# First row tile loaded in two column halves, and the imaginary operand's first piece put ahead of the second row tile

## The chip, the cores and the metric

The kernel runs on one core of one Trainium2 chip. The metric is the device time of one execution in microseconds. All inputs and outputs are fp32 and lie in the chip's memory (HBM) when the kernel starts.

## The reference

```python
xn = _layernorm(x, axis=-1)                    # x: 2048 x 640, normalised along each row
a = jnp.einsum("bsd,ed->bse", xn, dft_hid_re)  # DFT along the hidden dimension
b = jnp.einsum("bsd,ed->bse", xn, dft_hid_im)
s = jnp.einsum("ts,bse->bte", dft_seq_re, a) - jnp.einsum("ts,bse->bte", dft_seq_im, b)
g = _silu((_silu(xn @ w_gate) * (xn @ w_up)) @ w_down)   # 640 -> 1536 -> 640
return x + s * g
```

The sequence matrices are 2048 x 2048, the hidden ones 640 x 640.

## The kernel before

The work is three chains of matrix products. `seq` multiplies the two sequence matrices with the normalised rows, `hid_s` multiplies what comes out with the hidden matrices, and `gate_up` and `down` do the feed-forward part. All large products are built with Strassen's scheme of seven half-size products. Each fp32 operand is split into a high part, written by ScalarE (ACT), and a low part, the rest, written by VectorE (DVE). A product of a 128 x 128 weight tile and 128 x 512 moving columns is then three fast passes on TensorE (PE): high by high, high by low, low by high.

A planner (`Plan`) sets the order of the instructions. Each piece of work is given with a due time, the buffers that it reads and writes, and a cost. `schedule` turns this into one list in order of time, and each engine gets its instructions in that order. For the opening the due times are written out by hand, in the tables `OPEN_DMA`, `OPEN_LN`, `OPEN_T` and `OPEN_S` (lines 730 to 739), as us from the start of the real work.

The opening (`opening`, line 855) is the part the change touches. It computes the first of the seven products for the real and for the imaginary sequence matrix at once, over eight row tiles of x (128 rows by 640 columns each). For each row tile kk there are two blocks of products, one with the real operand (i = 0) and one with the imaginary (i = 1). The left operands come in pieces of 512 KB, each for two row tiles. This text calls the row tiles x0, x1, x2 and so on (320 KB each), and the pieces re0, re1 (real, for row tiles 0 and 1, then 2 and 3) and im0, im1 (imaginary). In `OPEN_DMA` a single number is a row tile and a pair is a piece: `(0, 0)` is re0, `(1, 0)` is im0, `(0, 1)` is re1.

What happens to a row tile: two statistics on DVE, one for each half of its columns (`bn_stats`, in the profile BATCH_NORM_STATS2), their aggregate, a root on ACT, some small steps on DVE (all in `layer_norm`), the normalisation on ACT (xn<-xn), and the split of its columns into high (ACT, hl<-xn) and low parts (DVE, hl<-xn). The operand pieces are split too (hl<-raw, ACT and DVE). Row tile 0 is an exception: its products are done in full precision without a split (PE ps<-raw and ps<-raw,xn), two instructions each. Six such instructions use re0 and six use im0, and then row tile 1 begins with split operands (PE ps<-hl), 18 products for each row tile. Before all this PE runs eleven products on a tile of zeros (`busy`, ps<-z) as filler.

All loads of the opening are issued by SyncE (SP) on one queue. Eight completion semaphores are used in turn, so each transfer issues only when the eighth before it has landed. In the order of before, SP's issue for x5 waits for re0, the next ones wait for x1, im0, x2, x3 and re1 in that order.

Each engine's instruction is recorded by one helper, so nearly all have the line number L82.

Of the kernel before, what the change touches and what calls it, by code (L numbers as in the profile page):

```python
# [14 lines left out]
P = 128  # L15
# [263 lines left out]
def tile_fnet_swiglu(  # L279
# [16 lines left out]
    nc = Probe(tc.nc)  # L296
# [5 lines left out]
    pl = Plan()  # L302
    mv = one.tile([P, NS, 2], F32, name="mv")
    sm = one.tile([P, 6, NS], F32, name="sm")
    bst = one.tile([P, 2, 2, 6], F32, name="bst")
# [9 lines left out]
    def raw(name, a=0, n=None):  # L315
        o, (arena, size) = where[name], pl.size[name]
        n = size - a if n is None else n
        over = arena == "raw" and o >= RAW_KB * 256 - 8
        return space["raw3" if over else arena][:, o + a - over * (RAW_KB * 256 - 8):][:, :n]
# [235 lines left out]
    xn = pl.buf(("xn",), "raw2", NS * D)  # L555
# [5 lines left out]
    def xn_tile(k):  # L561
        return space["xn", k // 8][:, k % 8 * D:k % 8 * D + D]

    def load_x(k, lead, eng):
        pl.prod(lead, lambda: eng.dma_start(xn_tile(k), x[k * P:(k + 1) * P, :]), [], [(xn, k)])

    def layer_norm(k0, n, lead, root, stats, small):

        for k in range(k0, k0 + n):
            for h in range(2):
                pl.prod(stats[k - k0], lambda k=k, h=h: nc.vector.bn_stats(
                    bst[:, k % 2, h], xn_tile(k)[:, h * 320:h * 320 + 320]), [(xn, k)], [("bst", k % 2, h)])
            pl.prod(stats[k - k0], lambda k=k: nc.vector.bn_aggr(
                mv[:, k], bst[:, k % 2].rearrange("p a b -> p (a b)")),
                [("bst", k % 2, 0), ("bst", k % 2, 1)], [("mv", k)])
        y, t, mr, v, nm = (sm[:, i, k0:k0 + n] for i in range(5))
        mean, var = (mv[:, k0:k0 + n, i] for i in range(2))  # L580
        r = rowst[:, 0, NS + k0:NS + k0 + n]
        key = ("sm", k0)
        if small is nc.vector and n == 1:
            sign, half = (-1.0, nm) if k0 == 0 else (1.0, r)
            ops = [
                lambda: nc.scalar.activation(t, var, AF.Sqrt, bias=sm[:, 5, 4:5], scale=0.25),
                lambda: nc.gpsimd.tensor_scalar(v, var, EPS, 0.25 * sign, op0=ALU.add, op1=ALU.mult),
                lambda: small.reciprocal(y, t),
                lambda: small.scalar_tensor_tensor(v, v, y, t, op0=ALU.mult, op1=ALU.subtract if k0 == 0 else ALU.add),
                lambda: small.reciprocal(half, v),  # L590
            ]
            if k0:
                ops.append(lambda: small.scalar_tensor_tensor(mr, mean, -1.0, r, op0=ALU.mult, op1=ALU.mult))
        elif small is nc.vector:
            stt = small.scalar_tensor_tensor
            ops = [
                lambda: nc.scalar.activation(t, var, AF.Sqrt, bias=sm[:, 5, :1]),
                lambda: small.reciprocal(y, t),
                lambda: stt(t, var, EPS, y, op0=ALU.add, op1=ALU.mult),
                lambda: stt(t, t, -0.5, y, op0=ALU.mult, op1=ALU.mult),  # L600
                lambda: stt(r, t, 1.5, y, op0=ALU.add, op1=ALU.mult),
                lambda: stt(mr, mean, -1.0, r, op0=ALU.mult, op1=ALU.mult),
            ]
        else:
            ops = [
                lambda: small.tensor_scalar(v, var, EPS, 1.0, op0=ALU.add, op1=ALU.mult),
                lambda: small.tensor_tensor(y, v, sm[:, 5, 8:8 + n], op=ALU.pow),
                lambda: small.tensor_scalar(nm, mean, -1.0, 0.0, op0=ALU.mult, op1=ALU.add),
                lambda: small.tensor_tensor(t, v, y, op=ALU.mult),
                lambda: small.tensor_tensor(t, t, y, op=ALU.mult),  # L610
                lambda: small.tensor_scalar(t, t, -0.5, 1.5, op0=ALU.mult, op1=ALU.add),
                lambda: small.tensor_tensor(r, y, t, op=ALU.mult),
                lambda: small.tensor_tensor(mr, nm, r, op=ALU.mult),
            ]
        for i, fn in enumerate(ops):
            pl.prod(root[i > 0], fn, [("mv", k) for k in range(k0, k0 + n)], [key])
        if k0 == 0:
            neg = pl.buf(("neg",), "raw", 256)
            minus = lambda to, a, n, scale: small.tensor_scalar(to, xn_tile(0)[:, a:a + n], mean, scale, op0=ALU.subtract, op1=ALU.mult)
            for e in range(2):  # L620
                pl.prod(root[2], lambda e=e: minus(raw(neg, e * P, P), e * P, P, nm), [(xn, 0), key], [(neg, 0)])
            pl.prod(root[2], lambda: small.tensor_scalar(r, nm, -1.0, 0.0, op0=ALU.mult, op1=ALU.add), [key], [key])
            pl.prod(root[2], lambda: minus(xn_tile(0)[:, TC:], TC, P, r), [(xn, 0), key], [(xn, 0, 2)])
            pl.prod(root[2], lambda: small.tensor_tensor(mr, mean, nm, op=ALU.mult), [key], [key])
            pl.prod(lead[0], lambda: nc.scalar.activation(
                xn_tile(0)[:, :TC], xn_tile(0)[:, :TC], AF.Identity, bias=mr, scale=r), [key, (xn, 0), (neg, 0)], [(xn, 0, 0), (xn, 0, 1)])
            return neg
        for k in range(k0, k0 + n):
            pl.prod(lead[k - k0], lambda k=k: nc.scalar.activation(
                xn_tile(k), xn_tile(k), AF.Identity, bias=sm[:, 2, k:k + 1], scale=rowst[:, 0, NS + k:NS + k + 1]),  # L630
                [key, (xn, k)], [(xn, k, c) for c in range(3)])
# [96 lines left out]


    OPEN_DMA = ((0,), (0, 0), (1,), (1, 0), (2,), (3,), (0, 1), (1, 1), (4,), (5,), (0, 2), (1, 2), (6,), (7,), (0, 3), (1, 3))  # L730
    OPEN_LN = ((0, 1, (-2.5,), (-1.4, -1.0, -0.5), (0.4,)),
               (1, 1, (0.5,), (1.6, 1.9), (2.8,)),
               (2, 1, (3.5,), (5.0, 5.3), (6.1,)),
# [8 lines left out]
    def seq(k):  # L742
# [112 lines left out]
        def opening():  # L855
# [3 lines left out]
            at = lambda t: -t  # L859
# [7 lines left out]
            def fetch(i, g, t, a=None):  # L867
                src = cs[j, i, g // 2, :, 2 * (g % 2):2 * (g % 2) + 2]
                name = left[i, g]
                if a is None:  # L870
                    pl.prod(at(t), lambda: nc.sync.dma_start(wide(raw(name)), src), [], [(name, 0), (name, 1)])
                else:
                    pl.prod(at(t), lambda: nc.sync.dma_start(raw(name, a * TC, TC), src[:, a]), [], [(name, a)])

            t = -6.0
            for what in OPEN_DMA:
                if len(what) == 1:
                    load_x(what[0], at(t), nc.sync)
                else:
                    fetch(what[0], what[1], t, *what[2:])  # L880
                t += 0.45
            neg = [layer_norm(k0, n, [at(x) for x in apply], [at(x) for x in root], [at(x) for x in stats], nc.vector)
                   for k0, n, stats, root, apply in OPEN_LN][0]
            for kk in range(1, 8):
# [9 lines left out]
            for kk in range(8):  # L894
                for i, banks, db in part if kk < 7 else part[::-1]:
# [6 lines left out]
                    o, a = (s[i, 1], 0) if kk == 1 else (s[i, kk // 2 * 2], kk % 2)  # L902
# [23 lines left out]
        def p2(g):  # L926
            if fresh:
                for kk in (8 + 2 * g, 9 + 2 * g):
                    load_x(kk, 40 + 2 * g, nc.sync)
                layer_norm(8 + 2 * g, 2, *LEAD["xn", 4 + g], nc.gpsimd)  # L930
            return operand("p2", g, load(12, g, 11 if fresh else 20, "raw"))
# [19 lines left out]
        if fresh:  # L951
            opening()
        elif not shared:
            run(("p1", p1, b2, (1, 1)))
# [467 lines left out]
```

## Time and profile before

| | |
|---|---|
| median of 3 runs | 969.66 us (969.62 to 969.9) |
| profiled execution, its own time | 969.83 us |
| span in it | 967.6 us |
| TensorE busy | 961.7 us, 99% of the span |
| VectorE, ScalarE, GpSimd busy | 734.6, 488.6, 121.3 us |
| granted TensorE clock | 0.999 |
| first real product | 6.46 us |

All times in the text are us from the start of the span unless it says otherwise. The profile's matmul rows overlap, since a product starts while the one ahead of it drains, so waits on TensorE are read from the spacing of starts. In the timeline a row gives start, length, engine, line and operation, the tiles written and read, and a count; a bracket gives the idle time of the engine ahead of the row and what ended it.

### The profile page before, as it was taken

The page shows a single profiled execution, that of the slowest core. Times are in us where ns is not written, and L with a number is a line of the kernel's source. Part 1 is how long each engine was busy: PE and PEld are TensorE (multiplying, and loading weights), DVE is VectorE, ACT ScalarE, POOL GpSimd, SP SyncE. Part 2 cuts the span into 40 slices and gives each one's busy share as a digit, 9 for nine tenths or more (in the row PEclk, how much of TensorE's full clock was granted, in tenths as well). Part 3 has the DMA queues.
Part 4 walks back from the last instruction along what each step waited for, and adds up shares of the span by engine and source line. Part 5 has one row for each costly group of instructions (what it writes and reads, how often), then busy time and mean ns, then how long its engine had stood idle before and what let it go on. Part 6 is the DMA issues. An engine that isn't in the chain of part 4 may idle for free.

```text
span 967.6 us, 11521 instructions
## 1 busy us (share of the span) xinstructions
PE 961.7 (99%) x4235; PEld 792.0 (82%) x4235; DVE 734.6 (76%) x932; ACT 488.6 (50%) x676; POOL 121.3 (13%) x184
## 2 busy tenths in 40 slices
PE   9999999999999999999999999999999999999998
PEld 5888888888888888888888888888888888888887
DVE  7889668757774687676987898999978666666775
ACT  5686445454545455544356555563446444444341
POOL 1460211011101110111100211210002000000000
PEclk9999999999999999999999999999999999999999
DMA  9997848494938497778673374439699330105793
GB/s 352 283 249 215 233 147 229 152 271 106 231 109 255 109 236 263 208 196 253 170 213 131 141 265 155 168 136 289 222 292 256 99 133 4 55 1 163 240 346 131
DMA packets 64056, 186.50 MB, mean 193 GB/s; under 512 B 6528, under 2 KB 10368, under 8 KB 64000
## 3 DMA queue, kind: packets, MB, share of 16 engines
q1 hardware_dynamic: 45952, 125.45, 39.0%
q0 software_dynamic: 18048, 60.32, 24.2%
q8 instruction: 33, 0.54, 0.2%
q14 instruction: 23, 0.19, 0.1%
HBM read 151.39 MB, written 34.36 MB: 192 GB/s over the span
## 4 chain that ended last, share of the span: by engine, by line
PE 99%; DMA 0%; DVE 0%; ACT 0%; issue 0%; DVEq 0%; ACTq 0%
PE ps L82 99%; DMA xn<-in_x 0%; DVE raw L82 0%; DVE bst L82 0%; DVE sm L82 0%; ACT raw L82 0%; ACT sm L82 0%; DVE mv L82 0%; DVEq L82 0%; ACTq L82 0%
## 5 line engine op out<-in xcount | busy, mean ns | idle before, releaser
L82 PE MATMUL ps<-hl 128*128 128x512 f32 (+1 forms) x3258 | 780.1, 388 | 0.0
L82 PEld LDWEIGHTS ps<-hl 128*128 128x128 f32 x3258 | 610.1, 188 | 126.6 <-DVE hl L82 0.6
L82 DVE TENSOR_TENSOR hl<-raw,hl 128x1024 fp32r<-128x1024 f32 (+5 forms) x360 | 346.5, 994 | 134.3 <-ACT hl L82 94.4
L82 ACT ACTIVATE hl<-raw 128x1024 fp32r<-128x1024 f32 (+6 forms) x416 | 325.0, 826 | 170.3 <-DVE raw L82 84.8
L82 PE MATMUL ps<-hl,hl 128*128 128x512 f32 (+1 forms) x954 | 259.9, 388 | 0.0
L82 ACT ACTIVATE raw<-ps 128x512 f32<-128x512 f32 (+1 forms) x144 | 97.9, 681 | 231.4 <-PE ps L82 225.2
L82 PEld LDWEIGHTS ps<-hl,hl 128*128 128x128 f32 x954 | 179.0, 188 | 36.9
L82 DVE TENSOR_TENSOR raw<-raw 128x1024 f32<-128x1024 f32 (+7 forms) x216 | 178.6, 849 | 19.8 <-ACT raw L82 15.5
L82 DVE TENSOR_TENSOR raw<-ps,raw 128x512 f32<-128x512 f32 (+1 forms) x95 | 77.2, 814 | 48.4 <-PE ps L82 47.6
L82 DVE TENSOR_TENSOR raw<-raw,raw 128x512 f32<-128x512 f32 (+3 forms) x50 | 44.2, 892 | 6.5 <-ACT raw L82 4.3
L82 ACT ACTIVATE hl<-xn 128x1024 fp32r<-128x1024 f32 (+3 forms) x61 | 42.2, 723 | 13.6 <-PE ps L82 9.1
L82 POOL DMA_DIRECT2D p_dram<-raw x24 | 16.4, 686 | 251.4 <-DVE raw L82 215.7
L82 ACT ACTIVATE raw<-raw 128x512 f32<-128x512 f32 (+1 forms) x30 | 21.5, 718 | 46.7 <-DVE raw L82 46.7
L82 DVE TENSOR_TENSOR hl<-xn,hl 128x1024 fp32r<-128x1024 f32 (+3 forms) x50 | 40.8, 833 | 4.0 <-PE ps L82 3.9
L82 POOL DMA_DIRECT2D raw<-in_cs x36 | 32.5, 984 | 57.7 <-DMA raw<-in_cs 29.1
L82 DVE SCALAR_TENSOR_TENSOR hl<-raw,hl 128x256 fp32r<-128x256 f32 (+4 forms) x56 | 32.7, 586 | 4.0 <-ACT hl L82 4.0
L82 POOL DMA_DIRECT2D out<-raw x10 | 6.9, 689 | 226.6 <-DVE raw L82 197.3
L82 POOL DMA_DIRECT2D d_p<-hl x28 | 15.2, 543 | 71.4 <-ACT hl L82 59.6
L82 ACT ACTIVATE xn<-xn,sm,rowst 128x640 f32<-128x640 f32 (+1 forms) x16 | 14.1, 906 | 5.3 <-DVE sm L82 3.6
L82 DVE BATCH_NORM_STATS2 bst<-xn 128x6 f32<-128x320 f32 x32 | 13.7, 479 | 4.0 <-DMA xn<-in_x 4.0
L82 POOL DMA_DIRECT2D y_dram<-raw x12 | 8.2, 683 | 64.6 <-DVE raw L82 46.2
L82 POOL DMA_DIRECT2D raw<-p_dram x8 | 10.1, 1267 | 44.7 <-DVE raw L82 26.3
(42 smaller groups left out, 84.3 us busy)
## 6 DMA issues: line engine op xcount, KB each, us to landing
raw<-in_cs SPq DMA_DIRECT2D x84, 512.0 KB, 7.0
hl<-d_p SPq DMA_DIRECT2D x56, 384.0 KB, 5.0
raw<-in_cs POOLq DMA_DIRECT2D x36, 512.0 KB, 9.8
raw<-in_wb SPq DMA_DIRECT2D x24, 640.0 KB, 4.7
d_p<-hl POOLq DMA_DIRECT2D x28, 384.0 KB, 4.0
p_dram<-raw POOLq DMA_DIRECT2D x16, 512.0 KB, 4.4
raw<-p_dram SPq DMA_DIRECT2D x8, 768.0 KB, 8.5
xn<-in_x SPq DMA_DIRECT2D x16, 320.0 KB, 9.8
```

The lines of the kernel that those rows point to most:

```text
L82: return real(*args, **kw)
```

## The change

It does two things, both in the opening. x0 is loaded by two transfers, columns 0 to 319 and columns 320 to 639, and each of its two statistics depends on its own half alone; whatever else reads x0 depends on both. And in `OPEN_DMA` im0 moves ahead of x1, and re1 ahead of x3.

```diff
+    pl.alias[xn, 0] = [(xn, 0, "a"), (xn, 0, "b")]
...
+    def load_x(k, lead, eng, h=None):
+        if h is None:
+            pl.prod(lead, lambda: eng.dma_start(xn_tile(k), x[k * P:(k + 1) * P, :]), [], [(xn, k)])
+        else:
+            pl.prod(lead, lambda: eng.dma_start(xn_tile(k)[:, h * 320:h * 320 + 320], x[k * P:(k + 1) * P, h * 320:h * 320 + 320]),
+                    [], [(xn, k, "ab"[h])])
...
-                    bst[:, k % 2, h], xn_tile(k)[:, h * 320:h * 320 + 320]), [(xn, k)], [("bst", k % 2, h)])
+                    bst[:, k % 2, h], xn_tile(k)[:, h * 320:h * 320 + 320]), [(xn, k) if k else (xn, k, "ab"[h])], [("bst", k % 2, h)])
...
-    OPEN_DMA = ((0,), (0, 0), (1,), (1, 0), (2,), (3,), (0, 1), (1, 1), (4,), (5,), (0, 2), (1, 2), (6,), (7,), (0, 3), (1, 3))
+    OPEN_DMA = ((0,), (0, 0), (1, 0), (1,), (2,), (0, 1), (3,), (1, 1), (4,), (5,), (0, 2), (1, 2), (6,), (7,), (0, 3), (1, 3))
...
+                if len(what) == 1 and what[0] == 0:
+                    for h in range(2):
+                        load_x(0, at(t + 0.2 * h), nc.sync, h)
```

On SP, at the start of the program, the order changes as follows. `xn_108<-in_x` is a row tile (128x320 is one of x0's halves) and `raw<-in_cs` a piece of a left operand; lines with a minus are before's, with a plus the change's, the others stand in both.

```order
-L82 DMA xn_108<-in_x 128x640
+L82 DMA xn_108<-in_x 128x320 x2
+L82 DMA raw<-in_cs 128x1024 x2
+L82 DMA xn_108<-in_x 128x640 x2
 L82 DMA raw<-in_cs 128x1024
 L82 DMA xn_108<-in_x 128x640
 L82 DMA raw<-in_cs 128x1024
-L82 DMA xn_108<-in_x 128x640 x2
-L82 DMA raw<-in_cs 128x1024 x2
```

Read from the top, SP issued x0, re0, x1, im0, x2, x3, re1, im1; now it issues x0's two halves, re0, im0, x1, x2, re1, x3, im1. There is one transfer more, so every later one takes the next semaphore in turn, and each still waits for the eighth ahead of it: im1 for x0's first half, x4 for its second.

On DVE, at the start of the program, no instruction moves. Only what the first statistics wait for changes; the names in the brackets are the semaphores of SP's transfers by their turn (DMAHW0, DMAHW1) and of the engines.

```order
 L82 BN_STATS bst<-xn_108 128x6 [waits DMAHW0_49]
-L82 BN_STATS bst<-xn_108 128x6
+L82 BN_STATS bst<-xn_108 128x6 [waits DMAHW1_49]
 L82 BN_AGGR mv<-bst 128x2 [waits DVE_49]
 L82 RECIPROCAL sm<-sm 128x1 [waits Activation_49]
```

The first statistic now waits for x0's first half alone and the second for the second half. The rest of DVE's order and that of ACT, PE and GpSimd stand as they were.

More of the change, by code (lines that the diff above doesn't have):

```diff
@@ L562, in xn_tile @@
         return space["xn", k // 8][:, k % 8 * D:k % 8 * D + D]
-    def load_x(k, lead, eng):
-        pl.prod(lead, lambda: eng.dma_start(xn_tile(k), x[k * P:(k + 1) * P, :]), [], [(xn, k)])
+    pl.alias[xn, 0] = [(xn, 0, "a"), (xn, 0, "b")]
[5 more added lines that the diff above has]
+                    [], [(xn, k, "ab"[h])])
     def layer_norm(k0, n, lead, root, stats, small):
@@ L876, in opening @@
             for what in OPEN_DMA:
-                if len(what) == 1:
+                if len(what) == 1 and what[0] == 0:
+                    for h in range(2):
+                        load_x(0, at(t + 0.2 * h), nc.sync, h)
+                elif len(what) == 1:
                     load_x(what[0], at(t), nc.sync)
```

## The prediction

> **What bounds the kernel now.** I read the page first: the span, the busy times and the chain that ended last.
>
> ```profile
> span 967.6 us, 11521 instructions
> PE 961.7 (99%) x4235; PEld 792.0 (82%) x4235; DVE 734.6 (76%) x932; ACT 488.6 (50%) x676; POOL 121.3 (13%) x184
> ```
>
> Then the chain in order of time. It shows one serial piece before TensorE takes over for good, and nothing but TensorE up to the last results:
>
> ```profile
> 0.73 3.01 DMA xn<-in_x
> 3.76 0.90 DVE bst L82 x2
> 6.06 0.36 DVE raw L82
> 6.46 956.86 PE ps L82 x4224
> ```
>
> The first row tile (x0) lands at 0.73 + 3.01 = 3.74, its two statistics take 0.90, and the first real product starts at 6.46. A chain hides short gaps, so next come the timeline of TensorE (start, length, count) and that of its weight loads, where a bracket gives the idle time ahead of the row and what ended it:
>
> ```profile
> 1.31 4.87 PE L82 MATMUL ps<-z 128*128 128x512 bf16 x11 [1.31 <-POOL sm L82]
> 16.06 367.63 PE L82 MATMUL ps<-hl 128*128 128x512 f32 x1620
> ...
> 6.46 0.30 PEld L82 LDWEIGHTS ps<-raw 128*128 128x128 f32 x2 [1.19 <-DVE raw L82]
> 7.85 0.19 PEld L82 LDWEIGHTS ps<-raw,xn 128*128 128x128 f32 x1 [0.24 <-issue]
> 8.28 0.19 PEld L82 LDWEIGHTS ps<-raw,xn 128*128 128x128 f32 x1 [0.24 <-issue]
> 9.25 0.30 PEld L82 LDWEIGHTS ps<-raw 128*128 128x128 f32 x2 [0.78 <-DMA raw<-in_cs]
> 11.93 4.09 PEld L82 LDWEIGHTS ps<-hl 128*128 128x128 f32 x18 [0.24 <-DVE hl L82]
> 16.42 0.76 PEld L82 LDWEIGHTS ps<-hl 128*128 128x128 f32 x4 [0.40 <-DVE hl L82]
> ```
>
> From 16.06 on, 1620 products take 367.63 us, 0.227 each with no room for a wait, and the same pace holds to the end by the 99%. So TensorE loses time in three places only, all in the opening: until 6.46 (x0's chain), at 9.25 (the first imaginary operand, im0) and at 16.42 (DVE's low part of the second real operand, re1). Full-precision loads stand 8.28 - 7.85 = 0.43 apart, and six of them are one half of row tile 0: 6 x 0.43 = 2.57, but 9.25 - 6.46 = 2.79, so the wait for im0 costs 0.22, not the 0.78 in the bracket. What matters for the end is one number: when the load now at 16.42 can issue. Every us there is a us at the end.
>
> Next the queue. SP issues each transfer after the eighth before it has landed, so from the ninth on its issue times give landings:
>
> ```profile
> 1.63 0.42 SPq L82 DMA_DIRECT2D xn<-in_x  x1
> 2.10 0.43 SPq L82 DMA_DIRECT2D raw<-in_cs  x1
> ...
> 5.26 0.48 SPq L82 DMA_DIRECT2D xn<-in_x  x1
> 6.87 0.33 SPq L82 DMA_DIRECT2D raw<-in_cs  x1
> 9.22 0.33 SPq L82 DMA_DIRECT2D raw<-in_cs  x1
> 10.25 0.33 SPq L82 DMA_DIRECT2D xn<-in_x  x1
> 11.00 0.33 SPq L82 DMA_DIRECT2D xn<-in_x  x1
> 12.24 0.33 SPq L82 DMA_DIRECT2D raw<-in_cs  x1
> ```
>
> In order: re0 landed at 5.26, x1 at 6.87, im0 at 9.22, x2 at 10.25, x3 at 11.00, re1 at 12.24. All was issued long before it landed, and the DMA engines were full (the two columns at the end of each window are DMA share and GB/s):
>
> ```profile
> 5.20:9.20 4.00, 3.72 (x9) 1.13 (x7) 3.12 (x14) 1.80 (x4) 0.19 (x1) 1.00 0.96 288
> 9.20:13.00 3.80, 3.80 (x12) 2.13 (x12) 3.35 (x13) 2.99 (x6) 0.25 (x1) 1.00 1.03 416
> ```
>
> So a transfer that moves ahead delays the one it passes by its own length.
>
> **Part 1, x0 in halves: about -0.38 at the first product.** It adds one issue on SP. x3 came 0.75 after x2, so 320 KB take about 0.75 and half of it 0.37: the first half lands near 3.37 (estimate from these rows) and its statistic (0.45) ends near 3.82. The second half, the same bytes in all, lands at 3.74 at best; at worst it is an issue later (2.10 - 1.63 = 0.47), 4.21. The second statistic starts then at 3.82 to 4.23, against 3.76 + 0.45 = 4.21 now. The gain lies between 0.39 and nothing (-0.02); I take 0.38, because the engines are the limit and the issue is not. TensorE can use it only where the eleven filler products are done: their row ends at 1.31 + 4.87 = 6.18, so 0.28 for certain, and up to 0.42 as the next product may start while the last one drains. Everything behind on SP is issued 0.47 later, or waits on another predecessor (im1, now ninth, waits for the first half, long landed), and that costs nothing while the backlog in the two windows above covers it.
>
> **Part 2, im0 ahead of x1: -0.22.** im0 will land right behind re0. With re1's length (12.24 - 11.00 = 1.24) that is 6.5, with its own measured 9.22 - 6.87 = 2.35 it is 7.6; both are before 8.85 (9.25 less part 1's 0.38, and 0.02 to spare for the wait), so that wait goes. Parts 1 and 2 would bring TensorE to row tile 1 at 11.93 - 0.60 = 11.33.
>
> **Part 3, what is late next: x1.** It passes behind 512 KB. Together im0 and x1 now take 9.22 - 5.26 = 3.96. If that sum is kept, x1 lands at 9.2 instead of 6.87. If both go at the later rows' speed (1.24 + 0.75 = 1.99), it lands at 7.25. I take 9.0: the sum in the same stretch of time is the nearest row, with a little off because the slow part may belong to the mixing of the two streams. This is the term on which the forecast stands.
>
> Who waits for x1: its statistics on DVE, and behind them in DVE's order everything for row tiles 1 and 2; ACT's rows likewise.
>
> ```profile
> 7.09 0.88 DVE L82 BATCH_NORM_STATS2 bst<-xn 128x6 f32<-128x320 f32 x2
> 11.18 0.21 DVE L82 BATCH_NORM_AGGREGATE mv<-bst 128x2 f32<-128x12 f32 x1
> 11.30 0.37 DVE L82 SCALAR_TENSOR_TENSOR hl<-xn,hl 128x256 fp32r<-128x256 f32 x1
> 13.20 0.88 DVE L82 BATCH_NORM_STATS2 bst<-xn 128x6 f32<-128x320 f32 x2
> 14.12 0.21 DVE L82 BATCH_NORM_AGGREGATE mv<-bst 128x2 f32<-128x12 f32 x1
> 14.61 0.42 DVE L82 SCALAR_TENSOR_TENSOR hl<-xn,hl 128x256 fp32r<-128x256 f32 x1 [0.28 <-ACT hl L82]
> 15.15 1.22 DVE L82 TENSOR_TENSOR hl<-raw,hl 128x1024 fp32r<-128x1024 f32 x1
> ...
> 9.49 0.92 ACT L82 ACTIVATE xn<-xn,sm,rowst 128x640 f32<-128x640 f32 x1 [0.95 <-DVE sm L82]
> 11.48 0.28 ACT L82 ACTIVATE sm<-mv,sm 128x1 f32<-128x1 f32 x1
> 12.25 1.06 ACT L82 ACTIVATE hl<-raw 128x1024 fp32r<-128x1024 f32 x1 [0.49 <-DMA raw<-in_cs]
> 13.22 0.91 ACT L82 ACTIVATE xn<-xn,sm,rowst 128x640 f32<-128x640 f32 x1
> 14.16 0.42 ACT L82 ACTIVATE hl<-xn 128x256 fp32r<-128x256 f32 x1
> ```
>
> Call S the start of x1's statistics: 7.09 now, x1's landing plus 0.02 after. ACT reaches x2's root at S + 4.39 (11.48) and is free at S + 4.67. Now it then idles 0.49 for re1. After, re1 has passed x3 and lands about 0.75 earlier, near 11.5, and that idle time goes: re1's high part at S + 4.67, x2's normalisation 0.97 later (13.22 - 12.25) at S + 5.64, the high part of its 256 columns 0.94 later at S + 6.58, done at S + 7.00. DVE meanwhile does x3's statistics at S + 6.11 (13.20), aggregates at S + 7.03 (14.12), and can start x2's low part 0.12 later (as 11.18 to 11.30), S + 7.15; it comes to re1's low part 0.54 later (15.15 - 14.61), S + 7.69, and ends it 1.22 later, S + 8.91. The load comes 0.05 behind, as 16.42 stands behind 16.37. So the load now at 16.42 comes at x1's landing + 8.98: the shift is x1's landing - 7.44. At 9.0 it is +1.56.
>
> Parts 1 and 2 do not lower this: TensorE reaches row tile 1 at 11.33 and waits for x1's first high part, which ends at S + 3.77 (10.44 + 0.42 now), near 12.8, so their 0.60 turn into waiting. From there 18 products (4.09) bring it to 17.0, where it waits again until 17.98. Later row tiles land as before, since the same bytes lie ahead of them.
>
> **Sum.** -0.38 and -0.22 absorbed, +1.56 at the load of 16.42, nothing behind it: 969.83 (the profiled execution's own time, 967.6 of it span) + 1.56 = 971.39. The median of the runs is 0.17 lower, 969.66, so 971.2. That is 0.16% more. About 0.2%, 1.94 us, is what a measurement of this kernel can tell from no change, so the forecast counts as no change, leaning to slower.
>
> **Rivals.** *The transfers go at full speed (15%, within 0.2%).* If im0 and x1 run at the 416 GB/s of the second window, their 852 KB take 2.05 and x1 lands at 7.3; the load of 16.42 then comes 0.1 earlier. In between, up to a landing at 8.2, the shift is at most +0.8. The time lies between 969.4 and 970.4; for it speaks that the windows after 9.2 hold that speed, against it the 288 GB/s of the window concerned. The Trainium skill's page "HBM Reference", section "Specifications (TRN2)", gives a core that streams alone about 425 GB/s; by that figure x1 would land near 7.3 by my estimate and the time be about 969.5. The trace agrees after 9.2 and not before.
>
> *Slower beyond 0.2%: im0 straight behind re0 is slower still (14%).* Two streams of the same shape meet without x1 between. It decides when x1 lands after 9.38 (7.44 + 1.94); at 9.7 the time is 971.9. For it speaks im0's 2.35 against re1's 1.24; against it that no row shows the pair above 3.96.
>
> *Slower: the clock falls while TensorE waits (7%).* The filler took 4.87 / 11 = 0.44 a product against 0.227 later, so there is a half-speed state, and the end of the trace shows it coming back (the column before the DMA share is the granted clock):
>
> ```profile
> 963.30:965.40 2.10, 0.01 (x1) 1.00 0.32 125
> 965.40:967.60 2.20, 0.00 (x0) 0.50 0.18 63
> ```
>
> About 2.1 us of idleness brought it. The change makes a wait of 12.9 - 11.33 = 1.6, close but shorter. If it happens, a half-speed stretch as long as the filler's (4.9) loses 2.4, of which the second wait covers about 1.0: 971.2 + 1.4 = 972.6. The Trainium skill's page "TensorE: Matmul & The Clock Gate", Part 1, says the clock halves after at least one idle window of about 3.4 us; by that rule this wait is too short and the time stays 971.2, while the trace's 2.1 us suggest that a partly idle window can do.
>
> *Faster beyond 0.2% (2%).* The three waits hold 0.42 + 0.22 + about 0.25 in all, under 1.94, so only something unseen could.
>
> **Chances.** The forecast's case, x1 landing between 8.2 and 9.38, holds 62%: 970.4 to 971.6. With the full-speed rival that makes 77% within 0.2%, 21% slower, 2% faster. The range runs from 969.6, which leaves out about 5% of the fast end, to 972.2, which leaves out the dropped clock and the extreme of a slower pair.
>
> **What would show it.** Right: x0's second statistic starts near 3.8 and the first product near 6.1; the load at 9.25 moves to about 8.7 with no DMA named; x1's statistics start near 9.0; weight loads wait over 1 us for `hl` near 11.3 to 12.9 and again near 18.0; from there 0.227 a product. Wrong: x1's statistics before 8.2 or after 9.4, a granted clock below 1 after 7 us, or a wait for a DMA later than 20 us.

## The result and the profile after

| | before | after |
|---|---|---|
| median | 969.75 us (969.62 to 969.9) | 973.98 us (973.81 to 975.17, 6 runs) |
| ratio, 95% interval | | 1.0047 (1.0037 to 1.0057) |
| profiled execution, its own time | 969.83 us | 974.96 us |
| span in it | 967.6 us | 972.7 us |
| last product ends (chain) | 963.32 | 967.60 |
| from there to the span's end | 4.3 | 5.1 |

The change costs 4.2 us in the median, where 1.5 were forecast. Four of the six runs lie near 973.9 (973.81 to 974.02), two near 975.1; the profile is of one of the two, so it shows about 1 us more than the median run has. Its chain of work that ended last reads, in order of time (start, length, what):

```profile
2.58 8.29 DMA xn<-in_x
10.88 0.90 DVE bst L82 x2
14.71 952.89 PE ps L82 x4212
```

Before, the chain began with x0, and TensorE was its own limit from 6.46 on. Now it begins with x1: it lands at 2.58 + 8.29 = 10.87, its statistics follow, and TensorE takes over at 14.71 only. The last product ends 967.60 - 963.32 = 4.28 later. The span grew by 5.1, so 0.8 more lies behind the last product. In the timeline of VectorE, ScalarE and TensorE after the change the opening reads:

```profile
3.07 0.89 DVE L82 BATCH_NORM_STATS2 bst<-xn 128x6 f32<-128x320 f32 x2 [3.07 <-DMA xn<-in_x]
5.37 0.61 DVE L82 TENSOR_SCALAR raw<-xn,mv,sm 128x128 f32<-128x128 f32 x2
...
7.27 0.63 ACT L82 ACTIVATE hl<-raw 128x512 fp32r<-128x512 f32 x1 [2.67 <-DMA raw<-in_cs]
...
7.38 1.95 PE L82 MATMUL ps<-raw 128*128 128x512 f32 x4 [1.22 <-DMA raw<-in_cs]
...
10.13 0.30 PEld L82 LDWEIGHTS ps<-raw 128*128 128x128 f32 x2 [0.76 <-DMA raw<-in_cs]
14.71 0.30 PEld L82 LDWEIGHTS ps<-hl 128*128 128x128 f32 x2 [2.57 <-ACT hl L82]
15.24 4.87 PEld L82 LDWEIGHTS ps<-hl 128*128 128x128 f32 x15 [0.23 <-DVE hl L82]
```

The halves do what they say: the statistics start at 3.07 instead of 3.76, and VectorE's step that the first product waits for (raw<-xn,mv,sm) at 5.37 instead of 6.06, both 0.69 earlier. But the first product starts at 7.38, held by re0, which lands at 7.25 (the ACT row starts 0.02 behind it; before, re0 landed at 5.24). Then TensorE waits for im0 again (10.13), and 2.57 for x1's high part (14.71). In the last row 15 loads take 4.87, where 18 took 4.09 before. The windows of that stretch say why (the number ahead of the last two is the granted clock):

```profile
12.00:14.70 2.70, 0.97 (x3) 0.14 (x1) 2.13 (x9) 1.67 (x4) 0.19 (x1) 1.00 1.04 420
14.70:16.30 1.60, 1.59 (x7) 1.17 (x8) 1.24 (x6) 1.60 (x4) 0.26 (x1) 0.99 1.01 410
16.30:19.70 3.40, 3.40 (x10) 2.63 (x9) 3.34 (x9) 3.00 (x6) 0.26 (x1) 0.50 1.04 421
19.70:22.00 2.30, 2.30 (x12) 1.89 (x11) 2.12 (x7) 1.38 (x3) 0.00 (x0) 1.00 1.02 419
```

After the wait the clock is half for 3.4 us. The end of the program is told by SyncE's list of waits (waited for: us in total, times, longest), before first, then after:

```profile
SPq L1418 <- DMA out<-raw: 0.7, 1, 0.7
...
SPq L1427 <- DMA out<-raw: 1.5, 1, 1.5
```

SP waits 1.5 instead of 0.7 for the last store, though that store takes equally long (1.91 and 1.88 from issue to landing). The accounts of the profiled execution are then (the clock's part is what the others leave over): x1's landing, 10.87 - 7.44 = 3.43 by the prediction's formula; the clock, the rest of the 4.28, 0.85; the end, 0.82; together 5.1, and 974.96 - 969.83 = 5.13.

### The profile page after: what moved, and what is told of

Read it like the earlier page. It is cut to its first block, busy times and chain, and to the rows that moved or that the text cites. A ratio compares the mean times of both kernels' runs of the same rounds, so it can differ in the third digit from the quotient of the medians.

```text
span 972.7 us, 11522 instructions
## 1 busy us (share of the span) xinstructions
PE 963.3 (99%) x4235; PEld 793.1 (82%) x4235; DVE 734.5 (76%) x932; ACT 488.3 (50%) x676; POOL 120.2 (12%) x184
## 4 chain that ended last, share of the span: by engine, by line
PE 98%; DMA 1%; DVE 0%; ACT 0%; SPq 0%; issue 0%; DVEq 0%
PE ps L82 98%; DMA xn<-in_x 1%; SPq L82 0%; ACT xn L82 0%; DVE bst L82 0%; DVE raw L82 0%; DVE sm L82 0%; ACT hl L82 0%; ACT raw L82 0%; ACT sm L82 0%; DVE mv L82 0%; DVE rowst L82 0%; DVEq L82 0%
## 5 line engine op out<-in xcount | busy, mean ns | idle before, releaser
L82 POOL DMA_DIRECT2D raw<-in_xt x6 | 6.9, 1296 | 72.3 <-DVE raw L82 72.3
```

The costliest lines, as they stand in the source:

```text
L82: return real(*args, **kw)
```

## The experiments

Time is the median, with the ratio to before (969.67 to 969.75 in these runs) and its 95% interval. "Product end" is the end of the last product in the profile (before: 963.3), "tail" the time from there to the span's end (before: 4.3). Each kernel has one trace, and a profiled execution can lie up to 1 us off its kernel's median: in e2, e8 and e13 it is the fastest run, 0.5 to 0.8 under the median, in e1 and the change 0.5 to 1.0 above it.

### The two parts apart

**e1**, the halves alone:

```diff
-    OPEN_DMA = ((0,), (0, 0), (1, 0), (1,), (2,), (0, 1), (3,), ...
+    OPEN_DMA = ((0,), (0, 0), (1,), (1, 0), (2,), (3,), (0, 1), ...
```

> Only x0 is split in halves; the order of the pieces and row tiles is that of the kernel before. Theory A (re0 and im0 running back to back slow each other): re0 lands near 5.3 and x1 near 6.9 as before, the first product starts near 6.1, and the time is 0.2 to 0.4 us under the kernel before, about 969.4. Theory B (the halves themselves leave some transfer engines late): re0 lands at 6.5 or later although x1 stands behind it, the first product starts at 6.6 or later, and the time is at or above 970.0.

Measured: 971.40, 1.0019 (1.001 to 1.0028); product end 964.59, tail 5.1. The part that was to cost nothing costs 1.7 in the median. Its chain starts with im0, which lands late because re0 did:

```profile
2.57 8.08 DMA raw<-in_cs
10.70 953.90 PE ps L82 x4218
```

**e2**, the order alone (the kernel before with the order of the change, x0 whole):

```diff
-    OPEN_DMA = ((0,), (0, 0), (1,), (1, 0), (2,), (3,), (0, 1), ...
+    OPEN_DMA = ((0,), (0, 0), (1, 0), (1,), (2,), (0, 1), (3,), ...
```

> Only the order changes (im0 ahead of x1, re1 ahead of x3); x0 is loaded whole. Theory A (the pair re0, im0): re0 lands near 7 and x1 near 10.8 as with the whole change, the granted clock drops once behind the wait, and the time is 973.5 to 974.5. Theory B (the halves): re0 lands near 5.3, x1 near 9.0 to 9.2, no drop of the clock, and the time is 971.2 to 971.7.

Measured: 971.76, 1.0022 (1.0013 to 1.0031); product end 964.74, tail 4.3. This is the prediction's own case: im0 is waited for no more, and x1 lands at 2.11 + 6.79 = 8.90, where 9.0 was taken. (That execution took 971.25; the median is 0.5 above it, and no trace shows where those runs have it.) Its chain, then those of four other kernels with the new order (whole change filled, whole change packed, order packed, change with seven more, all below):

```profile
2.11 6.79 DMA xn<-in_x
17.84 946.91 PE ps L82 x4193
...
2.57 7.36 DMA xn<-in_x
18.88 946.93 PE ps L82 x4193
...
2.58 5.48 DMA xn<-in_x
17.01 946.89 PE ps L82 x4193
...
2.10 6.06 DMA xn<-in_x
17.10 946.89 PE ps L82 x4193
...
2.58 7.04 DMA xn<-in_x
18.56 946.89 PE ps L82 x4193
```

x1's landings are 8.90, 9.93, 8.06, 8.16 and 9.62. The formula (landing - 7.44) gives +1.46, +2.49, +0.62, +0.72, +2.18 for the load of 16.42. It comes at +1.42, +2.46, +0.59, +0.68, +2.14, and from there on the length is the same in all. So the formula holds within 0.04 over a range of 1.9 us.

### Why the halves make re0 late

**e5**, two transfers of x0 by rows instead of columns (64 rows each, lines of 2560 bytes instead of 1280), both statistics waiting for both, order of before (lines with a minus are the change's):

```diff
-            pl.prod(lead, lambda: eng.dma_start(xn_tile(k)[:, h * 320:h * 320 + 320], x[k * P:(k + 1) * P, h * 320:h * 320 + 320]),
+            pl.prod(lead, lambda: eng.dma_start(xn_tile(k)[h * 64:h * 64 + 64, :], x[k * P + h * 64:k * P + h * 64 + 64, :]),
```

> x0 in two transfers again and the order of the kernel before, but split by rows: 64 rows of whole 2560-byte lines each, and both statistics wait for both. If the small pieces of 1280 bytes (or the engines left in step by them) make re0 late: re0 lands near 5.3 as before and the time is 969.6 to 969.9. If one more transfer ahead of re0 does it (re0 issued 0.47 later): re0 lands at 6 or later, the first product starts at 6.6 or later, and the time is 971 to 971.6, as with column halves.

Measured: 971.88, 1.0025 (1.0014 to 1.0035); product end 964.19, tail 5.1. The time is no better, and the windows below show the DMA engines partly idle as in e1, so short lines are not the cause of that. The first product comes at 7.09 here because x0 itself is late: its second part lands at 4.30.

**e9**, halves by columns in the order of before, the second issued by ACT at the same time, so that SP issues re0 as early as before (ACT's first table load moves behind it):

```diff
-                        load_x(0, at(t + 0.2 * h), nc.sync, h)
+                        load_x(0, at(t + 0.01 * h), (nc.sync, nc.scalar)[h], h)
```

> Column halves of x0 in the order of the kernel before, but the second half is issued by ACT ahead of its table load, at the same time as SP issues the first, so that re0 is issued at 1.16 as in the kernel before. If the postponed issue of re0 is what the halves cost (transfer engines run dry between x0 and re0): no dip in the share of the transfer engines between 3 and 4 us, re0 lands near 5.3, the first product starts near 6.1, and the time is 969.3 to 969.8. If the small pieces or the changed start do it: re0 at 6 or later and 971 or more, as with both halves on SP.

Measured: 970.61, 1.0009 (1.0 to 1.0018); product end 963.34, tail 5.18. The opening costs nothing now, and gains nothing: x0's halves land at 3.60 and 3.77. Before, the whole landed at 3.74; in e1 the halves landed at 3.03 and 3.43. When re0 is there, by ACT's first step on it, in e1, e5 and e9:

```profile
7.19 0.63 ACT L82 ACTIVATE hl<-raw 128x512 fp32r<-128x512 f32 x1 [2.61 <-DMA raw<-in_cs]
...
6.16 0.63 ACT L82 ACTIVATE hl<-raw 128x512 fp32r<-128x512 f32 x1 [0.23 <-DMA raw<-in_cs]
...
5.46 0.63 ACT L82 ACTIVATE hl<-raw 128x512 fp32r<-128x512 f32 x1 [0.31 <-DMA raw<-in_cs]
```

And two windows of half a us just where x0 ends and re0 goes on (DMA share and GB/s at the end), for before, e1, e5 and e9 in turn:

```profile
3.00:3.50 0.50, 0.50 (x3) 0.23 (x2) 0.00 (x0) 0.00 (x0) 0.00 (x0) 1.00 1.04 377
3.50:4.00 0.50, 0.50 (x3) 0.22 (x2) 0.24 (x1) 0.00 (x0) 0.00 (x0) 1.00 1.01 319
...
3.00:3.50 0.50, 0.50 (x3) 0.22 (x2) 0.45 (x2) 0.00 (x0) 0.00 (x0) 1.00 0.73 122
3.50:4.00 0.50, 0.50 (x3) 0.21 (x2) 0.47 (x3) 0.00 (x0) 0.00 (x0) 1.00 0.67 229
...
3.00:3.50 0.50, 0.50 (x3) 0.23 (x2) 0.00 (x0) 0.00 (x0) 0.00 (x0) 1.00 0.77 235
3.50:4.00 0.50, 0.50 (x3) 0.21 (x2) 0.00 (x0) 0.00 (x0) 0.00 (x0) 1.00 0.68 215
...
3.00:3.50 0.50, 0.50 (x3) 0.23 (x2) 0.00 (x0) 0.00 (x0) 0.00 (x0) 1.00 1.15 364
3.50:4.00 0.50, 0.50 (x3) 0.22 (x2) 0.38 (x1) 0.00 (x0) 0.00 (x0) 1.00 1.02 344
```

With a second transfer of x0 ahead of it on SP, re0 is issued 0.47 later (0.83 in e5) and the DMA engines stand partly idle at 3 to 4 us; with re0 issued in time they are full. In bytes e1 falls short of before by (377 + 319 - 122 - 229) x 0.5 = 172 KB there, which is about half a us at before's rate (an estimate from these rows).

re0's full lateness differs, though: it lands at 5.94 to 7.25 in the six kernels with x0 in two transfers on SP and the pieces as in before, against 5.24 before. And single executions scatter: in the trace of e12 below, whose opening is that of before, re0 lands at 5.96. The landing records go a step further, since each transfer lands in 16 parts. In the change 14 of re0's 16 parts are there by 5.56 and the other two at 6.60 and 7.25; in e1 14 by 5.80, two at 6.94 and 7.17; in e3, e4, e5 and e13 the last one comes at 5.94 to 6.24. So what makes re0 2.0 late instead of 0.7 to 1.0 is two late parts of sixteen. Why those two are late is not settled.

**e4**, halves on SP, im0 behind x1, re1 ahead of x3:

```diff
-    OPEN_DMA = ((0,), (0, 0), (1, 0), (1,), (2,), (0, 1), (3,), ...
+    OPEN_DMA = ((0,), (0, 0), (1,), (1, 0), (2,), (0, 1), (3,), ...
```

> x0 in halves, im0 behind x1 as in the kernel before, and only re1 moved ahead of x3. Theory A: re0 near 5.3, x1 near 6.9, im0 near 9.2, so TensorE still waits for im0 at 9.25 and starts row tile 1 at 11.93; re1 lands near 11.5, the wait at 16.42 goes (0.25), and the time is 0.2 to 0.3 us under the kernel before, about 969.5. Theory B: re0 at 6.5 or later, and the time at or above 970.0.

Measured: 971.46, 1.0019 (1.001 to 1.0028); product end 963.87, tail 5.1. No better than e1 in its median.

### The clock

**e3**, the whole change with eight products on the tile of zeros behind row tile 0, where TensorE waits for x1 (i is 1 for the imaginary operand):

```diff
-    def product(todo, reads):
+    def product(todo, reads, fill=0):
...
+            busy(ps[:, 7], fill)
...
-                        product(todo, [(c, 0), (neg, 0), (xn, 0, 2)])
+                        product(todo, [(c, 0), (neg, 0), (xn, 0, 2)], 8 * i)
```

> The whole change, and eight products on the tile of zeros behind row tile 0's last product, so that TensorE is busy for about 1.7 us of its wait for x1. If the drop of the clock costs time: the clock stays full after 7 us, the load for re1's low part comes at x1's landing + 8.98, and the time is 0.7 to 1.0 us under the whole change, about 973.1. If the drop costs nothing because the operands are late anyway: the same time as the whole change, 973.8 to 974.0.

Measured: 973.16, 1.0041 (1.0028 to 1.0053), 0.8 under the change; product end 965.80, tail 5.1. The clock holds (first row), and the shift is x1's landing alone. But x1 lands 0.94 earlier than in the change's trace, so the 0.8 cannot be put down to the fill. The fill is not the only way to this, however: e13 below has the whole change, no fill, a wait as long, and its clock holds too (second and third row):

```profile
16.30:19.70 3.40, 3.08 (x13) 2.20 (x13) 3.18 (x11) 2.12 (x6) 0.25 (x1) 1.00 1.03 417
...
13.46 0.30 PEld L82 LDWEIGHTS ps<-hl 128*128 128x128 f32 x2 [2.54 <-ACT hl L82]
...
16.30:19.70 3.40, 3.09 (x14) 2.21 (x13) 3.18 (x10) 2.15 (x5) 0.26 (x1) 1.00 1.03 417
```

So the wait alone does not decide. Where it falls does, as the records of the granted clock show. In the change's trace the clock is full from 6.02, half from 16.26 and full again from 19.67: distances of 10.24 = 3 x 3.413 and 3.41. In before 959.145 = 281 x 3.413 lie between the first full clock and the drop at the program's end, and all 17 traces fit steps of this length. Now take each step and the share of it in which TensorE was busy by the profile. In the change the step from 12.85 to 16.26 has 1.67 of 3.41, 49%, and the clock halves at its end. In e13 the wait is cut otherwise: the step from 9.90 to 13.31 has 1.85 of 3.41, 54%, and nothing happens. Over the 17 traces every step at full clock with a share of 49% or less is followed by half clock (18 steps, 17 of them at the program's end), and none of the others is; the next higher share is 54%. So a step about half idle was enough here, and the same wait costs or does not by how the steps happen to lie: the first full clock comes at 4.39 to 7.24 in these traces.

In the change's profile the drop cost the 0.85 that the formula leaves over. The runs near 973.9 have no trace. They fit 974.96 - 0.85 = 974.11 as executions without a drop, and as well e3's 973.16 + 0.85 = 974.01 as executions with a drop and x1 0.94 earlier. Their mean granted clock, 0.998 in three (0.948 in the fourth, which nothing here explains) against 0.999 to 1.000 in e13 and in four of e3's five runs, leans to the second, but the half clock at the program's end alone makes 0.998 in e9 and e12. So how the median's shift divides between x1 and the clock stays open.

### The speed of the early transfers

A piece of a left operand has 4 KB of each 8 KB line. **e7** is before with the operand's copy in memory laid out in whole blocks of 512 KB; **e8** the change with it, **e10** the order alone with it:

```diff
-        return m.reshape(NC, TC, NS // CG, CG, P).transpose(0, 2, 4, 3, 1)
+        return m.reshape(NC, TC, NS // 2, 2, P).transpose(0, 2, 4, 3, 1)
...
-                src = cs[j, i, g // 2, :, 2 * (g % 2):2 * (g % 2) + 2]
+                src = cs[j, i, g]
```

> The kernel before, with the sequence matrices stored so that each 512 KB piece is one contiguous block (lines 4 KB apart instead of 8 KB); the transfers are the same in size, number and order. If the line spacing makes the first pieces slow: re0 lands near 4.9, im0 before 8.0, the wait at 9.25 goes, and the time is 969.2 to 969.5. If not: re0 5.2, im0 9.2, 969.7.

> The whole change with the pieces stored as contiguous blocks. If the line spacing makes the first pieces slow: re0 lands near 5, im0 near 6.5 and x1 near 7.5, the load for re1's low part comes near 16.4, and the time is 969.3 to 969.9. If not: re0 at 6 or later, x1 at 9.9 or later, 973 to 974.

> x0 whole, the changed order (im0 ahead of x1, re1 ahead of x3), and the sequence matrices stored in contiguous 512 KB blocks. If the lines 8 KB apart are what makes im0 long: im0 lands near 6.6 and x1 near 7.5, 7.44 by the formula is the break-even, so the time is 969.4 to 970.2, against 971.8 without the packing. If the order costs by itself: 971 or more.

Measured: e7 969.47, 0.9998 (0.9989 to 1.0007), product end 962.91; e8 971.98, 1.0023 (1.0014 to 1.0033), product end 963.88, tail 5.1; e10 970.36, 1.0007 (0.9998 to 1.0016), product end 963.98, tail 4.3. The window from 5.2 to 9.2 of the change (first row) and of the packed change (second):

```profile
5.20:9.20 4.00, 2.78 (x8) 0.97 (x7) 1.21 (x6) 1.33 (x2) 0.00 (x0) 1.00 0.94 306
...
5.20:9.20 4.00, 4.00 (x11) 1.75 (x10) 2.35 (x10) 1.44 (x2) 0.00 (x0) 1.00 1.01 388
```

In the same window before goes from 288 to 336 GB/s (e7) and the order alone from 319 to 351 (e10). So the slow early transfers come in part from the layout. Packed, x1 lands at 8.06 and 8.16, and the order shifts the load by 0.6 to 0.7 instead of 1.4. It never becomes a gain, because x1, behind im0, still lands later than 7.44.

### The end of the program

Every kernel above with one transfer more than before (265 on SP and ACT together, against 264 = 8 x 33) has a tail of 5.0 to 5.2, every other one 4.3. The trace's records of SP's last semaphore waits show a difference (when each wait is over, in us, and the number of the completion semaphore; 118 is not one of SP's):

```
before   965.09 118  965.15 100  965.21 103  965.28 104  965.36 106  965.44 107  965.51 108  965.87 109  966.61 110   span ends 967.61
change   969.37 118  970.92 100  970.98 101  971.04 104  971.13 106  971.21 107  971.57 108  971.65 109  971.71 110   span ends 972.72
```

At the end SP waits for its eight semaphores one by one, in the order of their numbers. Before, the last store was on 110, the last of them: the seven others were done while it was under way, and the span ended 1.02 behind its landing. The eight are used in turn, so one transfer more puts the last store on 100, the first: the seven others come after it, and the span ends 1.82 behind.

**e12**, the kernel before with one transfer of 2.5 KB from memory to memory at about 400 us; **e13**, the change with seven of them:

```diff
+    extra = dram.tile([8, D], F32, name="extra")
+    more = 1        # 7 in e13
...
+        if t >= 400 and more:
+            for _ in range(more):
+                nc.sync.dma_start(extra[more - 1:more], x[more - 1:more, :])
+                more -= 1
```

> The kernel before with one 2.5 KB transfer more on SP, from memory to memory, about 400 us into the program; nothing waits for it. Theory (the completion semaphores): the eight are used in turn, and at the end SP waits for every one of them in the order of their numbers; one transfer more puts the last store on the first of the eight instead of the last, so that the seven other waits follow its landing instead of preceding it. Then the last product ends as before (963.3 within 0.4), the span ends 5.1 behind it instead of 4.3, and the time is about 0.8 above before's. Rival (the 0.82 belongs to the opening, to the halves): the span ends 4.3 behind the last product and the time is before's within 0.2.

> The whole change with seven such small transfers more, eight more than before in all, so that the turn comes round to the same semaphore as before. Theory of the semaphores: the span ends 4.3 behind the last product instead of 5.13, and the time is about 0.8 below the change's, near 973.1. Rival (more transfers, longer end): the span ends 5.1 or more behind the last product, and the time is 974 or above. If the opening's clock drops or not is left to this run to show: with the drop, weight loads at half pace in 16 to 20 us and the last product near 967.6, without it near 966.6.

Measured: e12 970.35, 1.0006 (0.9997 to 1.0015), e13 973.13, 1.0035 (1.0021 to 1.0049). In the profiles, e12's products end at 963.11 and its last store is on 100, tail 5.4; e13's last store is on 110 again, tail 4.8. Counted from the landing of the last store, the span ends 2.11 later in e12 and 1.02 later in e13, the latter as before: the turn of the semaphores moves the end. One transfer that does nothing costs 0.6 in the median. e13's median is 0.85 under the change's, and in the profiles its tail is 0.3 shorter than the change's; how the rest divides between x1 and the clock no trace of a median run shows. Both tails are longer than expected by 0.3 to 0.5. In e13 the last store is issued 1.71 behind the last product instead of 1.40 and takes 2.11 to land instead of 1.88; in e12 the step behind SP's last wait takes 0.95 instead of 0.66. Why is not settled.

### A version that beats both?

**e6** is before with re1 ahead of x3 alone, **e15** that on packed blocks, x0 whole. **e11** is packed, with e9's halves and re1 ahead of x3; **e14** is e11 with one load of the last stage issued by POOL instead of SP, which takes the last store back to 110. The edits of e6 and of e14:

```diff
-    OPEN_DMA = ((0,), (0, 0), (1,), (1, 0), (2,), (3,), (0, 1), ...
+    OPEN_DMA = ((0,), (0, 0), (1,), (1, 0), (2,), (0, 1), (3,), ...
...
-            fold or pl.post(lambda: nc.sync.dma_start(
+            fold or pl.post(lambda: (nc.gpsimd if q == 21 and e == 0 else nc.sync).dma_start(
```

> The kernel before with one step of the order alone: re1 ahead of x3. x0 is whole and im0 stays behind x1. By the working of the prediction the wait at 16.42 goes and nothing else moves: 0.2 to 0.3 us under the kernel before, about 969.4. By the rival, that any new order of the first transfers costs by itself, 970.5 or more.

> What helped or cost nothing, joined: x0 in column halves with the second issued by ACT, re1 ahead of x3 with im0 left behind x1, and the matrices in contiguous 512 KB blocks. If the waits are additive: the first product near 6.1, x1 near 6.7, im0 before 8.7 so that no weight load waits for a transfer, the load for re1's low part near 15.7, and the time 968.8 to 969.2. If the starts are bound elsewhere: 969.4 to 969.7, as with the packing alone.

> Halves with the second one issued by ACT, re1 ahead of x3, the pieces stored as whole 512 KB blocks, and one load of the last stage (256 KB of in_xt) issued by POOL instead of SP, so that the eight semaphores have as many transfers as before. Theory of the semaphores: the last product ends near 963.0 as it did with all but the last of these edits, the span ends 4.3 behind it, and the time is 969.2 to 969.4, 0.3 to 0.5 under before's. Rival: the end stays 5.0 behind the last product and the time stays at 970.1.

> x0 whole, the kernel before's order except re1 ahead of x3, and the pieces stored as whole 512 KB blocks: no transfer more than before. The blocks alone brought the last product to 962.91 and the order of re1 alone to 963.08, against 963.30; together 962.6 to 962.9, the span ends 4.3 behind, the time 969.2 to 969.5. If it is no faster than the blocks alone (969.47), the opening has nothing left that an order of loads can take.

Measured: e6 969.79, 1.0001 (0.9992 to 1.0009); e11 970.07, 1.0005 (0.9996 to 1.0014); e14 969.33, 0.9998 (0.9989 to 1.0007), tail 4.5; e15 969.45, 0.9998 (0.9989 to 1.0007). The chains of e14 and e15 are before's, a little shorter:

```profile
6.36 956.50 PE ps L82 x4224
...
6.46 956.46 PE ps L82 x4224
```

Of e14's 0.74 under e11, 0.5 is the semaphore's turn once more (the span ends 1.23 instead of 1.73 behind the landing of the last store). Both beat the change by over 4.5 us; neither is told apart from before. Without the two later waits of the opening they end their last product 0.4 to 0.5 earlier than before, and more those waits do not hold.

## Why the prediction was wrong

**The bound** (right). The last product's end follows from when the load of 16.42 can issue; five kernels show it.

**Part 1, the halves** (wrong step: everything behind on SP "is issued 0.47 later", and "that costs nothing while the backlog ... covers it"). The two windows that were quoted for the backlog begin at 5.2; at 3 to 4 us, when x0 ends, no such backlog stands behind it: in e1 the engines fell to 0.7 of their time. In the change itself, where im0 follows re0 on SP, the dip is that of 3.0 to 3.5 (0.76) alone. The gain at VectorE was larger than sized, 0.69 against 0.38, because the second half did not land "at 3.74 at best" but at 3.43, ahead of a later re0; where re0 is issued in time (e9) the first step gains only 0.14. It was worth nothing, since re0 came 2.0 later and no term of the sum asked when re0 has to be there. Alone this part costs 1.3 in the opening (e1's profiled execution; the median of e1 is 0.5 lower). e9 takes the cost away by moving the second issue off SP's queue, so the issue ahead of re0 on that queue is the cause. It accounts for about half a us of the 2.0; why two parts of re0 come later still is open.

**Part 2, im0** (right alone, wrong in the whole). With x0 whole the wait goes (e2). With the halves re0 is late, im0 lands at 10.09 instead of the 6.5 to 7.6 of the prediction, and the load that was to come at 8.7 comes at 10.13.

**Part 3, x1** (mechanism right, size off). 9.0 was taken, and e2 gives 8.90. That is so close in part by luck: re0 landed 0.18 later than before, and im0 and x1 took 3.47 behind it where 3.74 was taken. In the whole change x1 lands at 10.87, because re0's lateness of 2.0 goes through im0 to x1: x1 comes 3.6 behind re0 there, 3.7 in e3 and 3.5 in e13. The term was +1.56; it measured +1.42 in the profile of the order alone, the fastest of its runs, and +3.43 in the profile of the change.

**The end** (not in the prediction). +0.82 from the last store's semaphore. The prediction counted the transfer's issue and the predecessor that each transfer waits for, and did not follow the turn of the eight to the program's end.

**The rivals.** Full speed did not come; packed blocks bring 388 GB/s and still +0.6, so its bound of +0.8 below a landing of 8.2 was right. The dropped clock came in the profiled execution, at 0.85 instead of 1.4, after a wait of 2.57 on the loads and 1.74 on the products. The prediction's suspicion that a partly idle window can do was right: 49% busy was enough, 54% was not. The Trainium skill's page "TensorE: Matmul & The Clock Gate", Part 1, has the clock halve after at least one idle window; with the word idle the traces disagree. The same section calls the window free-running, and with that they agree, as the first full clock at 4.39 to 7.24 shows.

The forecast of 971.2 stands 0.6 under the order alone (971.76), which is all that it described. What it left out are 1.3 to 2.0 for a late re0 (by profiles), 0.8 for the end, and in some executions the clock.

## What to carry to other kernels

Before splitting a transfer, look at the DMA share in the half microsecond behind it: where nothing is queued up there, one more issue on the queue delays the next transfer by more than the issue. Ask of each transfer in the queue, not only of the one split, when its reader needs it. And count transfers: where completion semaphores are used in turn and waited for in a fixed order at the end, one transfer more or less anywhere can move the end by 0.6 to 0.8 us, so compare ends of the last product beside times before crediting a gain or a loss to an edit. Where kernels differ by less than 1 us, compare the profiled execution with its own median before reading a difference of medians from it.

## What the runs showed of the hardware

- The granted clock changes in steps of 3.41 us. A step in which TensorE was busy 49% was followed by 3.41 us at half clock, one with 54% was not; waits of 2.57 and 2.54 us on its loads made the difference only by where they fell. With filler products in the wait the profiled execution kept its clock, though one of e3's five runs took 975.09, at a mean clock of 0.997, against 973.1 to 973.6 for the others.
- Splitting x0 by rows costs as much as by columns (971.88 and 971.40), so longer lines do not help.
- A transfer lands in 16 parts, and two late ones can hold up the whole: re0 in the change has 14 by 5.56 and the last at 7.25.
- Reading 4 KB out of lines of 8 KB is slower than whole blocks early on (from 5.2 to 9.2: 306 against 388 GB/s in the change, 288 against 336 in before), and not later (from 9.2 to 13.0 in before: 416 against 414).
- SP's waits at the program's end take 0.06 to 0.36 each, so the span ends 1.0 us (before) to 1.8 us (the change) behind the landing of the last store, by the store's semaphore.
